# Middle rows of a Fourier transform as two stationary tiles of high and low parts, in a fused FFT and feed-forward kernel

## The chip, the cores and the metric

The kernel runs on one core of one Trainium2 chip. The metric is the device time in microseconds of one execution; three runs of the kernel before stand below. One execution was recorded by the hardware profiler. The five engines are TensorE (PE, its weight loads PEld), VectorE (DVE), ScalarE (ACT), GpSimd (POOL) and SyncE (SP, which issues transfers).

## The reference

```python
X = np.fft.fft(x, axis=1); X = np.fft.fft(X, axis=2)   # x: 8 batches x 3072 x 256, fp32
y = X.real.astype(np.float32).reshape(8 * 3072, 256)
h = y @ w_in                                           # 256 -> 2048
g = np.maximum(h, 0.0) + alpha * np.minimum(h, 0.0)    # alpha: one number per hidden unit
out = (g @ w_out).astype(np.float32)                   # 2048 -> 256
```

## The kernel before

The transform over 3072 positions is reduced by sums and differences of mirrored rows ("folds") to small products of folded rows with cosine and sine tables. The transform over the 256 features is not computed by itself: it is multiplied into the first weight matrix. The folded results go to a tile `X`, as a high and a low part of each number.

**The feed-forward steps.** Columns of the result are worked on in blocks of 386, 384 or 512; a batch from 1 to 6 has three blocks of 512, batch 7 four of 386. A step is one block with one of 16 slices of the hidden layer. `ffn1` makes six products into two PSUM banks (lines L804 to L806), VectorE and ScalarE apply the activation (L822, L830, L834, L777), `split_parts` makes a high part `hi` on ScalarE (L783) and a low part `lo` on GpSimd (L785), and `ffn2` adds twelve products to four accumulators (L902). `ffn1` runs three steps ahead of `ffn2`. At the end of a block `evacuate` copies two accumulators by ScalarE (L931) and two by VectorE (L929); the next block's first products overwrite them. All products of this pair are in `float32r`, of high by high, high by low and low by high parts.

**The transforms beside them.** While the steps of batch b run, the transforms of batch b + 1 are prepared and run. `r` counts the steps of a batch, 0 to 47 where it has three blocks. GpSimd and VectorE do the folds at r = 4 to 36. The four even units (`see`, `cee`, `ceo`, `seo`) follow at r = 38, 40, 41, 42, the rows of the odd units are turned (`turn_rows`: six ScalarE copies `part` at L515, two GpSimd sums, `aco` or `aso` at L517 and `odds` at L518) at r = 44 and 46, and the two odd units, of two transforms each, run at r = 0 and 3 of the next batch. So a batch has eight transforms, four in even and four in odd units.

**One transform (`dft`).** A transform has 384 folded rows in three tiles of 128 and writes two column halves, even and odd, of 193 (or 192) columns side by side in one PSUM bank. Tile 0 feeds the even half only, tile 2 the odd half only. The middle tile feeds both: its lower 64 rows the even half, its upper 64 the odd half, and the table of the middle has zeros elsewhere. Tiles 0 and 2 are multiplied in fp32, which the profile shows as two passes per product (L603). The middle of batches 2 to 7 is multiplied in `float32r` (L600): three products of both halves together, 386 or 384 columns wide, by the pairs (high rows, high table), (high rows, low table), (low rows, high table). Some transforms add a product of four rows kept apart, `zres` by `res` (L599, 194 columns).

**Where the parts come from.** `parts` makes a `float32r` copy on ScalarE (L576, tile `mh`) and subtracts it from the fp32 numbers on GpSimd (L577, tile `ml`). `mids` calls it for the rows of an even unit pair at r = 37 and of the odd units at r = 44 (`co`) and 46 (`so`), behind `turn_rows`, on two groups of 128 rows by 128 columns each. `parts_table` does the same for the six tables once, at six steps of batch 1 (`TABLE_STEPS`).

**Order.** The schedule is written by hand: every engine works its own queue in the order in which the program issues. In a step the order is `ffn1` of three steps ahead, `ffn2`, the ScalarE copies of `evacuate` if a block ends, the activation (`pair`), the VectorE copies of `evacuate`; then the steps' transform work, as `turn_rows` and `mids`. The four banks of the pool `pq` rotate between `ffn1` and the transforms.

Of the kernel before, what the change touches and what calls it, by code (L numbers as in the profile page):

```python
# [10 lines left out]
F32 = mybir.dt.float32  # L11
# [76 lines left out]
def _tables():  # L88
    p = PI.reshape(3, P)
    j, i2 = np.arange(193)[None, :], np.arange(192)[None, :]  # L90

    def four(full):
# [9 lines left out]
    seo = four(s)  # L102
# [9 lines left out]
        ee=np.concatenate([cee, see], 1), eo=np.concatenate([ceo, seo], 1),  # L112
        er=np.concatenate([rca, rsb], 1), feat=feat, ident=ident,
    )
    return {k: np.ascontiguousarray(v, dtype=np.float32) for k, v in out.items()}


# [29 lines left out]
def fft2_prelu_ffn(ctx: ExitStack, tc: tile.TileContext, t, outputs):  # L147
    nc = tc.nc
# [34 lines left out]
    ee = tabs.tile([P, 8, 193], F32, name="ee")  # L183
    eo = tabs.tile([P, 8, 192], F32, name="eo")
    er = tabs.tile([P, 8, 193], F32, name="er")


    wih, wil = wts.tile([P, KF, 2, P], F32R, name="wih"), wts.tile([P, KF, 2, P], F32R, name="wil")
# [375 lines left out]
        )  # L564


    TABS = dict(cee=(ee, 0), see=(ee, 4), ceo=(eo, 0), seo=(eo, 4), ca=(er, 0), sb=(er, 4))
    middle = {}

    def parts(key, n, rows, places):  # L570

        tag = key if key in TABS else key[0]
        two = middle[key] = [late.tile([P, n], F32R, tag=f"m{tag}{h}", name="m" + h) for h in "hl"]
        for i, v in enumerate(rows):
            hi, lo = (places(m, i) for m in two)
            S.activation(out=hi, in_=v, func=ACTF.Copy)  # L576
            G.tensor_tensor(out=lo, in0=v, in1=hi.bitcast(F32), op=ALU.subtract)  # L577

    def parts_table(kind):
        tab, at = TABS[kind]  # L580
        v = tab[:, at + 2:at + 4].rearrange("p k n -> p (k n)")
        parts(kind, v.shape[-1], [_pairs(v)], lambda m, _: _halves(m))

    def dft(kind, v, zr, m, mid=None, bank=None):

        ps = (bank or other_bank())[0:m]
        tab, at = TABS[kind]
        n = tab.shape[-1]
        even, odd = [(v[:, 0], tab[:, at])], [(v[:, 2], tab[:, at + 1])]
        if mid is None:  # L590
            even.append((v[:, 1], tab[:, at + 2]))
            if zr is not None:
                even.append((zr.bitcast(F32), res[:, 0:n].bitcast(F32)))
            odd.append((v[:, 1], tab[:, at + 3]))
        else:
            (fh, fl), (th, tl) = mid, middle[kind]
            for i, (lhsT, rhs) in enumerate(((fh, th), (fh, tl), (fl, th))):
                if i == 2 and zr is not None:
                    nc.tensor.matmul(out=ps[:, 0:n + 1], lhsT=zr, rhs=res, start=False, stop=False)  # L599
                nc.tensor.matmul(out=_pairs(ps[:, 0:2 * n]), lhsT=lhsT, rhs=_halves(rhs), start=(i == 0), stop=False)  # L600
        for o, terms in ((0, even), (n, odd)):
            for i, (lhsT, rhs) in enumerate(terms):
                nc.tensor.matmul(  # L603
                    out=ps[:, o:o + n], lhsT=lhsT, rhs=rhs, start=(mid is None and i == 0),
                    stop=(i == len(terms) - 1 and (o > 0 or mid is None)),
                )
        return ps, n, m

    def dft_early(kind, v, zr):

        ps = other_bank()
        tab, at = TABS[kind]
        n = tab.shape[-1]
# [3 lines left out]
        terms += [(n, v[:, 1], tab[:, at + 3]), (n, v[:, 2], tab[:, at + 1])]  # L617
        for i, (o, lhsT, rhs) in enumerate(terms):
            if i in (1, len(terms) - 1):
                yield ps, n, P  # L620
            nc.tensor.matmul(
                out=ps[:, o:o + n], lhsT=lhsT, rhs=rhs, start=(i in (0, len(terms) - 2)), stop=(i in (len(terms) - 3, len(terms) - 1)),
            )

    def odd_sums(ps, n, m):
        os = foldp.tile([P, 193], F32, tag="os", name="os", bufs=2)[0:m, 0:n]
        S.activation(out=os, in_=ps[:, n:2 * n], func=ACTF.Copy)  # L627
        return ps, os, n, m

    def butterfly(ps, n, m):  # L630
# [9 lines left out]

    def mids(b, nm):

        low, high = rows_of(b, nm)
        rows = [low[:, 1] if nm[1] == "e" else turned[nm][:, 1], high[:, 1]]
        parts(nm, 2 * P, rows, lambda m, i: m[:, i * P:(i + 1) * P])

    def mid_of(nm, i):
        return [m[:, i * P:(i + 1) * P] for m in middle[nm]] if nm in middle else None

    def unit_odd(b, nm):  # L650

# [439 lines left out]
    for b in range(NB):  # L1091
# [3 lines left out]
        for r in range(len(mine) * KF):  # L1095
# [118 lines left out]
```

## Time and profile before

| | us |
|---|---|
| median of three runs | 1643.32 (1641.93 to 1643.6) |
| the profiled execution, own time | 1642.61 |
| its span, first to last instruction | 1640.8 |
| TensorE busy | 1626.6 (99%) |
| VectorE, GpSimd, ScalarE busy | 1455.2 (89%), 1292.4 (79%), 1131.3 (69%) |

The granted TensorE clock is 0.999 of full speed over the span. A matmul's record is longer than the time for which it holds the stream: records of successive matmuls overlap, so it is the distance between their starts that counts. In a row of the timeline several instructions of one group are merged; "x4" is their count, and the time is from the first start to the last end. Engine names with PEld are weight loads.

### The profile page before, as it was taken

What the parts mean: (1) busy time and instruction counts of PE and PEld (TensorE: products, weight loads), DVE (VectorE), ACT (ScalarE), POOL (GpSimd) and SP (SyncE); (2) the same over time, 40 slices, a digit from 0 to 9 for tenths busy, and PEclk for the clock granted to TensorE, in tenths of its full rate; (3) what the DMA queues carried; (4) which work ended last, traced back from release to release, by engine and by line L of the source; (5) the groups of instructions that cost most, each with busy time, mean ns of one, the idle gap of its engine ahead of it and who ended that gap; (6) DMA issues with size and microseconds to landing.
All of it is one profiled execution on the core that took longest, in us unless ns stands there. A gap on an engine that the chain in (4) does not pass through costs nothing.

```text
span 1640.8 us, 25922 instructions
## 1 busy us (share of the span) xinstructions
PE 1626.6 (99%) x8132; PEld 1455.1 (89%) x8132; DVE 1455.2 (89%) x2483; ACT 1131.3 (69%) x2094; POOL 1292.4 (79%) x1306
## 2 busy tenths in 40 slices
PE   8999999999999999999999999999999999999998
PEld 6779999888888888888888888888888888899998
DVE  7979988999899998999889998899988999889997
ACT  6876677667676667766676666766667666677775
POOL 4688987888788888888877888788878888776665
PEclk9999999999999999999999999999999999999999
DMA  6410210011000120010100101001100010000000
GB/s 238 135 53 6 63 65 20 20 59 52 20 33 28 45 71 1 33 52 33 59 27 7 63 22 59 26 8 71 52 20 26 20 46 32 1 31 25 25 20 21
DMA packets 25531, 69.28 MB, mean 42 GB/s; under 512 B 5722, under 2 KB 8114, under 8 KB 25394
## 3 DMA queue, kind: packets, MB, share of 16 engines
q1 hardware_dynamic: 25090, 67.45, 11.6%
q8 instruction: 65, 1.06, 0.3%
q14 instruction: 72, 0.59, 0.1%
q10 hardware_dynamic: 304, 0.17, 0.0%
HBM read 42.34 MB, written 25.26 MB: 41 GB/s over the span
## 4 chain that ended last, share of the span: by engine, by line
PE 93%; DVE 2%; POOL 1%; ACT 1%; issue 1%; DVEq 0%; POOLq 0%; ACTq 0%
PE acc L902 57%; PE pq L804 10%; PE pq L806 10%; PE pq L805 10%; PE ps L603 3%; PE acc L876 2%; PE ps L600 1%; PE ps L376 1%; DVE d L830 1%; POOL lo L785 1%; DVE pf L822 0%; DVE d L777 0%; ACT pq L834 0%; ACT part L515 0%; ACT hi L783 0%
## 5 line engine op out<-in xcount | busy, mean ns | idle before, releaser
L785 POOL TENSOR_TENSOR lo<-d,hi 128x512 fp32r<-128x512 f32 (+2 forms) x804 | 971.5, 1225 | 284.2 <-ACT hi L783 255.3
L783 ACT ACTIVATE hi<-d 128x512 fp32r<-128x512 f32 (+2 forms) x804 | 483.0, 601 | 356.2 <-DVE d L777 307.5
L777 DVE SCALAR_TENSOR_TENSOR d<-d,sg,pq 128x512 f32<-128x512 f32 (+2 forms) x804 | 565.6, 703 | 11.6 <-ACT pq L834 11.6
L834 ACT ACTIVATE pq<-d,sga 128x512 f32<-128x512 f32 (+2 forms) x832 | 541.4, 653 | 45.2 <-DVE d L830 44.3
L830 DVE TENSOR_TENSOR d<-pf,pq 128x512 f32<-128x512 f32 (+2 forms) x832 | 530.7, 641 | 8.5 <-POOL lo L785 0.4
L902 PE MATMUL acc<-hi,h 128*128 128x512 f32 (+2 forms) x1604 | 455.3, 365 | 1.1 <-ACT o L931 1.0
L822 DVE SCALAR_TENSOR_TENSOR pf<-xbc,w,pq 128x512 f32<-128x512 f32 (+2 forms) x416 | 299.0, 719 | 108.7 <-PE pq L806 100.9
L902 PE MATMUL acc<-lo,h 128*128 128x512 f32 (+2 forms) x1604 | 391.9, 364 | 0.0
L902 PE MATMUL acc<-hi,l 128*128 128x512 f32 (+2 forms) x1604 | 391.9, 364 | 0.0
L902 PEld LDWEIGHTS acc<-hi,h 128*128 128x128 f32 x1604 | 297.3, 189 | 34.7 <-ACT o L931 3.6
L902 PEld LDWEIGHTS acc<-lo,h 128*128 128x128 f32 x1604 | 294.6, 189 | 30.9
L902 PEld LDWEIGHTS acc<-hi,l 128*128 128x128 f32 x1604 | 294.6, 189 | 30.8
L804 PE MATMUL pq<-X,wih 128*128 128x512 f32 (+2 forms) x832 | 314.2, 378 | 3.3 <-DVE d L777 3.2
L806 PE MATMUL pq<-X,wil 128*128 128x512 f32 (+2 forms) x832 | 302.1, 363 | 1.5 <-DVE wil L392 1.5
L805 PE MATMUL pq<-X,wih 128*128 128x512 f32 (+2 forms) x832 | 301.9, 363 | 0.1
L804 PEld LDWEIGHTS pq<-X,wih 128*128 128x128 f32 x832 | 157.0, 189 | 26.2 <-PE pq L806 3.1
L806 PEld LDWEIGHTS pq<-X,wil 128*128 128x128 f32 x832 | 157.1, 189 | 17.6 <-DVE wil L392 2.0
L805 PEld LDWEIGHTS pq<-X,wih 128*128 128x128 f32 x832 | 157.2, 189 | 16.1 <-DVE X L701 0.3
L423 POOL TENSOR_TENSOR raw<-raw 128x512 f32<-128x512 f32 (+1 forms) x112 | 97.7, 873 | 0.0
L638 DVE TENSOR_TENSOR y<-ps,os 128x193 f32<-128x193 f32 (+3 forms) x68 | 21.1, 352 | 31.2 <-ACT os L627 31.2
L344 POOL TENSOR_TENSOR w<-we,wm 128x512 int32<-128x512 int32 (+1 forms) x18 | 21.2, 1180 | 33.6 <-DVE wm L334 17.3
L931 ACT ACTIVATE o<-acc 128x512 f32<-128x512 f32 (+2 forms) x50 | 25.5, 561 | 21.7 <-PE acc L902 21.7
(172 smaller groups left out, 916.6 us busy)
## 6 DMA issues: line engine op xcount, KB each, us to landing
raw<-in_xh SPq DMA_DIRECT2D x42, 512.0 KB
out<-o SPq DMA_DIRECT2D x36, 512.0 KB
raw<-in_w SPq DMA_DIRECT2D x16, 512.0 KB
xbc<-xcd SPq DMA_DIRECT2D x18, 256.0 KB
out<-o SPq DMA_DIRECT2D x8, 386.0 KB
before<-in_xh SPq DMA_DIRECT2D x6, 512.0 KB
out<-o SPq DMA_DIRECT2D x6, 384.0 KB
er<-in_er SPq DMA_DIRECT2D x1, 772.0 KB
```

The costliest lines, as they stand in the source:

```text
L423: yield size, lambda o=o, i0=i0, i1=i1, op=op: e.tensor_tensor(out=o, in0=i0, in1=i1, op=op)
L603: nc.tensor.matmul(out=ps[:, o:o + n], lhsT=lhsT, rhs=rhs, start=(mid is None and i == 0), stop=(i == len(terms) - 1 and (o > 0 or mid is ...
L777: V.scalar_tensor_tensor(out=g, in0=d, scalar=sg[:, f:f + 1], in1=ad, op0=ALU.mult, op1=ALU.max)
L783: S.activation(out=hi, in_=d, func=ACTF.Copy)
L785: G.tensor_tensor(out=lo, in0=d, in1=hi.bitcast(F32), op=ALU.subtract)
L804: nc.tensor.matmul(out=out, lhsT=wih[:, f, q], rhs=xh, start=True, stop=False)
L805: nc.tensor.matmul(out=out, lhsT=wih[:, f, q], rhs=xl, start=False, stop=False)
L806: nc.tensor.matmul(out=out, lhsT=wil[:, f, q], rhs=xh, start=False, stop=True)
L822: V.scalar_tensor_tensor(out=_pairs(pf), in0=_halves(xbc[g]), scalar=w128[:, f:f + 1], in1=_pairs(ps[0]), op0=ALU.mult, op1=ALU.add,)
L830: V.tensor_tensor(out=d, in0=pf, in1=ps[1], op=ALU.add if i else ALU.subtract)
L834: S.activation(out=ad, in_=d, func=ACTF.Copy, scale=sga[:, f:f + 1])
L902: nc.tensor.matmul(out=out, lhsT=wt[:, o * P:(o + 1) * P], rhs=rhs, start=(f == 0 and n[o] == 0), stop=(f == KF - 1 and n[o] == 2),)
```

## The change

For batches 2 to 7 the middle tile is no longer one tile of high and one of low parts of all 128 rows. It becomes two stationary tiles, `me` and `mo`. `me` holds the high parts of the lower 64 rows in partitions 0 to 63 and their low parts in partitions 64 to 127; `mo` holds the high parts of the upper 64 rows in partitions 64 to 127 and their low parts in 0 to 63. Each table half becomes two tiles of 194 (192) columns: the high part of its 64 rows in both partition halves, and the low part in both. A column half is then two products, with the high and with the low table, and a transform has four products of half the columns in place of three of all. All four pairs of parts are in them. The odd half starts at column 194 of the bank (192 where n is 192), and the tables `ee` and `er` are padded with a column of zeros.

The copies and subtractions change with it: each works on 64 partitions, the subtraction reads one partition half and writes the other, an odd unit's middle takes four of each instead of two, an even one's two of each on 256 columns, and a table two of each per column half, at twelve steps of batch 1.

```diff
-    def parts_table(kind):
-        tab, at = TABS[kind]
-        v = tab[:, at + 2:at + 4].rearrange("p k n -> p (k n)")
-        parts(kind, v.shape[-1], [_pairs(v)], lambda m, _: _halves(m))
+    LOWER, UPPER = slice(0, 64), slice(64, 128)
+
+    def parts_table(kind, o):
+
+        tab, at, n = TABS[kind]
+        own, other = ((LOWER, UPPER), (UPPER, LOWER))[o]
+        m = [late.tile([P, n + n % 2], F32R, tag=f"m{kind}{o}{h}", name="m" + h) for h in "hl"]
+        middle.setdefault(kind, []).append(m)
+        v = _pairs(tab[own, at + 2 + o])
+        for rows in (own, other):
+            S.activation(out=_halves(m[0][rows]), in_=v, func=ACTF.Copy)
+        for rows in (own, other):
+            G.tensor_tensor(out=_halves(m[1][rows]), in0=v, in1=_halves(m[0][own]).bitcast(F32), op=ALU.subtract)
...
-            (fh, fl), (th, tl) = mid, middle[kind]
-            for i, (lhsT, rhs) in enumerate(((fh, th), (fh, tl), (fl, th))):
-                if i == 2 and zr is not None:
-                    nc.tensor.matmul(out=ps[:, 0:n + 1], lhsT=zr, rhs=res, start=False, stop=False)
-                nc.tensor.matmul(out=_pairs(ps[:, 0:2 * n]), lhsT=lhsT, rhs=_halves(rhs), start=(i == 0), stop=False)
...
+        w = n + n % 2
+        for o in range(2):
+            out, wide = ps[:, w * o:w * o + n], ps[:, w * o:w * o + w]
...
+                terms += [(_pairs(wide), mid[o], _halves(m)) for m in middle[kind][o]]
+                if o == 0 and zr is not None:
+                    terms.append((ps[:, 0:n + 1], zr, res))
+                terms.append((out, v[:, 2 * o], tab[:, at + o]))
+            for i, (at_, lhsT, rhs) in enumerate(terms):
+                nc.tensor.matmul(out=at_, lhsT=lhsT, rhs=rhs, start=(i == 0), stop=(i == len(terms) - 1))
...
     def mids(b, nm):
 
-        low, high = rows_of(b, nm)
-        rows = [low[:, 1] if nm[1] == "e" else turned[nm][:, 1], high[:, 1]]
-        parts(nm, 2 * P, rows, lambda m, i: m[:, i * P:(i + 1) * P])
+        two = [late.tile([P, 2, P], F32R, tag=f"m{nm[0]}{o}", name="m" + o) for o in "eo"]
+        middle[nm] = [m[:, ::-1] if nm == "se" else m for m in two]
+        if nm[1] == "e":
+            at = 4 if nm == "ce" else 5
+            groups = [(slice(0, 2), even[:, at:at + 3:2])]
+        else:
+            groups = [(0, turned[nm][:, 1]), (1, rows_of(b, nm)[1][:, 1])]
+        for k, v in groups:
+            for m, own, other in ((two[0], LOWER, UPPER), (two[1], UPPER, LOWER)):
+                S.activation(out=m[own, k], in_=v[own], func=ACTF.Copy)
+                G.tensor_tensor(out=m[other, k], in0=v[own], in1=m[own, k].bitcast(F32), op=ALU.subtract)
...
-    TABLE_STEPS = (7, 11, 18, 22, 26, 30)
+    TABLE_STEPS = (5, 7, 9, 11, 13, 18, 20, 22, 24, 26, 28, 30)
...
-                parts_table(list(TABS)[TABLE_STEPS.index(r)])
+                parts_table(list(TABS)[TABLE_STEPS.index(r) // 2], TABLE_STEPS.index(r) % 2)
```

## Rows read from the trace of the kernel before

**Rows 1.** The page: busy time by engine, and the chain that ended last.

```profile
PE 1626.6 (99%) x8132; PEld 1455.1 (89%) x8132; DVE 1455.2 (89%) x2483; ACT 1131.3 (69%) x2094; POOL 1292.4 (79%) x1306
...
PE 93%; DVE 2%; POOL 1%; ACT 1%; issue 1%; DVEq 0%; POOLq 0%; ACTq 0%
```

**Rows 2.** The chain of waits in order of time: start us, us, what, count.

```profile
461.16 2.59 PE acc L902 x12
...
465.05 2.85 PE acc L902 x12
...
1250.15 2.82 PE acc L902 x12
```

**Rows 3.** Timeline of TensorE: start us, us, engine, line, out<-in, [idle before].

```profile
1445.87 0.92 PE L902 MATMUL acc<-hi,h 128*128 128x386 f32 x2 [0.72 <-ACT o L931]
```

**Rows 4.** All instructions of line L600: count, ns min/median/max, first and last start, forms.

```profile
L600 PE MATMUL ps<-mh x48: 326/327/462, 423.9 to 1460.9; 128*128 128x386 f32 x36, 128*128 128x384 f32 x12
...
L600 PE MATMUL ps<-ml,mh x48: 326/327/327, 424.1 to 1461.2; 128*128 128x386 f32 x36, 128*128 128x384 f32 x12
```

**Rows 5.** Timeline of TensorE, the products of one transform.

```profile
432.86 0.33 PE L600 MATMUL ps<-mh 128*128 128x386 f32 x1
433.03 0.33 PE L600 MATMUL ps<-ml,mh 128*128 128x386 f32 x1
433.19 0.25 PE L599 MATMUL ps<-res,zres 128*128 128x194 f32 x1
433.28 0.35 PE L600 MATMUL ps<-mh,ml 128*128 128x386 f32 x1
433.46 0.82 PE L603 MATMUL ps<-ee,even 128*128 128x193 f32 x4
```

**Rows 6.** Timeline of TensorE's weight loads, the same transform.

```profile
433.19 0.19 PEld L600 LDWEIGHTS ps<-mh,ml 128*128 128x128 f32 x1
433.30 0.68 PEld L603 LDWEIGHTS ps<-ee,even 128*128 128x128 f32 x4
```

**Rows 7.** Timeline of TensorE behind the `co` pair of batch 2.

```profile
470.57 0.38 PE L806 MATMUL pq<-X,wil 128*128 128x512 f32 x1
470.79 0.44 PE L804 MATMUL pq<-X,wih 128*128 128x512 f32 x1
```

**Rows 8.** Timeline of GpSimd, r = 44 to 46 of batch 1's block.

```profile
455.88 0.46 POOL L577 TENSOR_TENSOR ml<-aco,mh 128x128 fp32r<-128x128 f32 x1
456.35 0.46 POOL L577 TENSOR_TENSOR ml<-odds,mh 128x128 fp32r<-128x128 f32 x1
456.87 5.02 POOL L785 TENSOR_TENSOR lo<-d,hi 128x512 fp32r<-128x512 f32 x4
461.90 1.02 POOL L517 TENSOR_TENSOR aso<-odds,part 128x384 f32<-128x384 f32 x1
```

**Rows 9.** Timeline of ScalarE at the boundary of batches 1 and 2.

```profile
463.92 0.31 ACT L576 ACTIVATE mh<-odds 128x128 fp32r<-128x128 f32 x1 [0.66 <-POOL odds L518]
464.14 1.07 ACT L931 ACTIVATE o<-acc 128x512 f32<-128x512 f32 x2
```

**Rows 10.** Timeline of TensorE at the same boundary.

```profile
464.88 0.86 PE L902 MATMUL acc<-hi,h 128*128 128x512 f32 x2
```

**Rows 11.** Timeline of GpSimd at r = 37 of batch 1.

```profile
422.83 1.72 POOL L577 TENSOR_TENSOR ml<-even,mh 128x128 fp32r<-128x128 f32 x4
```

**Rows 12.** Timeline of GpSimd at the start.

```profile
1.34 0.88 POOL L257 MEMSET ee<- 64x386 f32 x2
...
2.17 0.41 POOL L278 MEMSET zres<- 128x384 f32 x1
```

**Rows 13.** GpSimd's groups by line and form: count, busy us, mean ns, idle before.

```profile
L423 POOL TENSOR_TENSOR raw<-raw 128x256 f32<-128x256 f32 x84 | 61.7, 735 | 0.0
```

**Rows 14.** Stretches: us, then busy us (count) of PE, PEld, DVE, ACT, POOL; clock, DMA.

```profile
296.28:331.25 34.97, 34.97 (x164) 30.62 (x163) 32.61 (x51) 24.21 (x39) 31.64 (x29) 1.00 0.05 16
346.79:397.29 50.50, 50.50 (x236) 44.22 (x235) 47.03 (x73) 35.44 (x57) 45.62 (x42) 1.00 0.08 27
```

More of the change, by code (lines that the diff above doesn't have):

```diff
@@ L114, in _tables @@
     )
+    for k in ("ee", "er"):
+        out[k] = np.concatenate([out[k], np.zeros((P, 8, 1))], 2)
     return {k: np.ascontiguousarray(v, dtype=np.float32) for k, v in out.items()}
@@ L181, in fft2_prelu_ffn @@
     dummy = work.tile([P, 512], F32R, tag="hi0", name="dummy", bufs=3)
-    ee = tabs.tile([P, 8, 193], F32, name="ee")
+    ee = tabs.tile([P, 8, 194], F32, name="ee")
     eo = tabs.tile([P, 8, 192], F32, name="eo")
-    er = tabs.tile([P, 8, 193], F32, name="er")
+    er = tabs.tile([P, 8, 194], F32, name="er")
     wih, wil = wts.tile([P, KF, 2, P], F32R, name="wih"), wts.tile([P, KF, 2, P], F32R, name="wil")
@@ L564, in load_rows_384 @@
         )
-    TABS = dict(cee=(ee, 0), see=(ee, 4), ceo=(eo, 0), seo=(eo, 4), ca=(er, 0), sb=(er, 4))
+    TABS = dict(
+        cee=(ee, 0, 193), see=(ee, 4, 193), ceo=(eo, 0, 192), seo=(eo, 4, 192), ca=(er, 0, 193), sb=(er, 4, 193),
+    )
     middle = {}
[L570 to L577, printed above, removed]
@@ L584, in dft @@
     def dft(kind, v, zr, m, mid=None, bank=None):
         ps = (bank or other_bank())[0:m]
[L587 to L595, printed above, removed]
-            (fh, fl), (th, tl) = mid, middle[kind]
-            for i, (lhsT, rhs) in enumerate(((fh, th), (fh, tl), (fl, th))):
-                if i == 2 and zr is not None:
-                    nc.tensor.matmul(out=ps[:, 0:n + 1], lhsT=zr, rhs=res, start=False, stop=False)
-                nc.tensor.matmul(out=_pairs(ps[:, 0:2 * n]), lhsT=lhsT, rhs=_halves(rhs), start=(i == 0), stop=False)
@@ L601, in dft @@
[L601 to L606, printed above, removed]
+        tab, at, n = TABS[kind]
+        tab = tab[:, :, 0:n]
+        w = n + n % 2
+        for o in range(2):
+            out, wide = ps[:, w * o:w * o + n], ps[:, w * o:w * o + w]
+            terms = []
+            if mid is None:
+                terms += [(out, v[:, 2 * o], tab[:, at + o]), (out, v[:, 1], tab[:, at + 2 + o])]
+                if o == 0 and zr is not None:
+                    terms.append((out, zr.bitcast(F32), res[:, 0:n].bitcast(F32)))
+            else:
+                terms += [(_pairs(wide), mid[o], _halves(m)) for m in middle[kind][o]]
+                if o == 0 and zr is not None:
+                    terms.append((ps[:, 0:n + 1], zr, res))
+                terms.append((out, v[:, 2 * o], tab[:, at + o]))
+            for i, (at_, lhsT, rhs) in enumerate(terms):
+                nc.tensor.matmul(out=at_, lhsT=lhsT, rhs=rhs, start=(i == 0), stop=(i == len(terms) - 1))
@@ L611, in dft_early @@
         ps = other_bank()
-        tab, at = TABS[kind]
-        n = tab.shape[-1]
+        tab, at, n = TABS[kind]
+        tab = tab[:, :, 0:n]
         terms = [(0, v[:, 0], tab[:, at]), (0, v[:, 1], tab[:, at + 2])]
@@ L616, in dft_early @@
             terms.append((0, zr.bitcast(F32), res[:, 0:n].bitcast(F32)))
-        terms += [(n, v[:, 1], tab[:, at + 3]), (n, v[:, 2], tab[:, at + 1])]
+        w = n + n % 2
+        terms += [(w, v[:, 1], tab[:, at + 3]), (w, v[:, 2], tab[:, at + 1])]
         for i, (o, lhsT, rhs) in enumerate(terms):
@@ L626, in odd_sums @@
         os = foldp.tile([P, 193], F32, tag="os", name="os", bufs=2)[0:m, 0:n]
-        S.activation(out=os, in_=ps[:, n:2 * n], func=ACTF.Copy)
+        S.activation(out=os, in_=ps[:, n + n % 2:2 * n + n % 2], func=ACTF.Copy)
         return ps, os, n, m
@@ L641, in mids @@
     def mids(b, nm):
-        low, high = rows_of(b, nm)
-        rows = [low[:, 1] if nm[1] == "e" else turned[nm][:, 1], high[:, 1]]
-        parts(nm, 2 * P, rows, lambda m, i: m[:, i * P:(i + 1) * P])
+        two = [late.tile([P, 2, P], F32R, tag=f"m{nm[0]}{o}", name="m" + o) for o in "eo"]
[3 more added lines that the diff above has]
+            groups = [(slice(0, 2), even[:, at:at + 3:2])]
+        else:
+            groups = [(0, turned[nm][:, 1]), (1, rows_of(b, nm)[1][:, 1])]
[3 more added lines that the diff above has]
+                G.tensor_tensor(out=m[other, k], in0=v[own], in1=m[own, k].bitcast(F32), op=ALU.subtract)
     def mid_of(nm, i):
-        return [m[:, i * P:(i + 1) * P] for m in middle[nm]] if nm in middle else None
+        return [m[:, i] for m in middle[nm]] if nm in middle else None
     def unit_odd(b, nm):
```

## The prediction, made before the changed kernel was run

> **What bounds the kernel now.** I read the page first: its busy times and its chain of waits [rows 1]. TensorE is busy for 99% of the span and 93% of the chain is its own work, so a change pays only by what it takes from TensorE's stream, and costs only where TensorE is made to wait. Next, the chain in order of time [rows 2]: the twelve second-layer products of a 512-column step take 2.59 us, 0.216 us each, step after step. At 465.05 they take 2.85. Five such rows stand in the trace, one at each of the first five batch boundaries (465, 661, 857, 1053 and 1250 us), each about 0.25 us too long. The sixth boundary idles longer, for 0.72 us in its row and behind one name: L931, ScalarE's copy of the finished accumulator [rows 3]. Between the boundaries TensorE is full. So two things are to be priced: the transforms' products, and what the new splits do to the copy at the boundary.
>
> **The products.** There are 48 transforms with a middle (six batches by eight), three `float32r` products each, 36 transforms at 386 columns and 12 at 384 [rows 4]. In the stream [rows 5] such products start 0.165 us apart (432.86, 433.03, 433.19), so three cost 0.49 us. The change puts four products of 194 (or 192) columns in their place. The trace holds one product of that width, L599 with 194 columns: from its start to the start of the second product behind it are 0.27 us, of which the 386-column one takes 0.165, so L599 holds the stream for 0.11 us, not half of 0.165. The load row tells why [rows 6]: the load that begins with L599 is followed 0.11 us later by the next load. Every product brings a load of 128 columns, also where the same stationary tile is used twice running (L600 has 48 loads for `ps<-mh` and 48 for `ps<-ml,mh` [rows 4]). A product shorter than 0.11 us costs 0.11.
>
> The Trainium skill says it too (TensorE: Matmul & The Clock Gate, section "LDWEIGHTS (loading the stationary operand)"): a load takes its column count over 1.2, 107 ns for 128 columns, however few rows are in use; the load rows agree. The same page's section "Back-to-back issue gap" gives columns over 2.4 plus 2.5 ns for the product alone, an estimated 83 ns at 194 columns; the stream here goes by the load.
>
> Four products are then 0.44 us against 0.49, and 0.05 us goes per transform, 2.4 us over 48. The fp32 products (two a transform) and L599 keep their number and width. Not all 2.4 us stay. Behind the `co` pair (r = 0 of a batch) TensorE already waits for a bank: the L804 row at 470.79 is 0.44 us long where its neighbours have 0.38 [rows 7]. That bank comes free by the chain that starts at the boundary, so there the 0.1 us a batch, 0.6 in all, only lengthens a wait. Kept: even units 24 x 0.05 = 1.2, `so` pairs 12 x 0.05 = 0.6, together 1.8 us.
>
> **The splits at the boundary.** Each middle of an odd unit is now written by four ScalarE copies and four GpSimd subtractions on 64 rows instead of two and two on 128. GpSimd's run [rows 8]: the subtractions `ml` at 455.88 and 456.35 (r = 44), then four `lo` in one unbroken run of 5.02 us from 456.87, then `aso` at 461.90, 0.01 us after it, and `odds` behind it. ScalarE [rows 9] copies `mh<-odds` at 463.92, after 0.66 us of waiting for that `odds`, and the accumulator copies follow in the same queue at 464.14, 1.07 us for both. TensorE's second product of the new block waits for the second one: its pair takes 0.86 us from 464.88, where two unhindered ones would end within 0.216 + 0.38 = 0.60 [rows 7, 10]. The whole chain thus runs through GpSimd, and nothing in it has slack: what is added on GpSimd at r = 44 arrives at TensorE at r = 48.
>
> Added there, by rows: a subtraction of 128 elements issued back to back costs 0.42 us (four `ml` in 1.72 us at 422.83 [rows 11], one alone is 0.46 long [rows 8]: 1.26 / 3). I take that for 64 partitions too, because a memset of 386 elements on 64 partitions takes as long as one of 384 on 128: two in 0.88 us against 0.41 for one [rows 12]. Four from 455.88 let `lo` start at 455.88 + 4 x 0.42 = 457.56, not 456.87: 0.69 us late. `aso` and `odds` inherit it. Then ScalarE has two copies instead of one behind `odds`; the second costs the 0.22 us between 463.92 and 464.14 [rows 9]. The accumulator copy comes 0.69 + 0.22 = 0.91 us later, and TensorE, which had no slack to it, waits 0.91 us more. The chain starts behind steps that TensorE itself paces, so an earlier TensorE shifts it all alike. Six boundaries (b = 1 to 6): 5.5 us. Behind them the queues and TensorE are late by the same amount, so nothing is won back.
>
> Bounds of this term. Below: half tiles could run beside each other on GpSimd, so that two cost what one does; then only ScalarE's copies count, once at r = 44 before `lo` and once before the accumulator copy, 0.22 + 0.22 = 0.44 a boundary, 2.6 us. Above: the result lies in the other 64 partitions, which no row shows; at the nearest dearer row, 0.735 us for 256 elements [rows 13], two extra and two dearer subtractions make `lo` late by 4 x 0.735 - 0.99 = 1.95 and the boundary by 2.2, 13 us over six. I take 0.91, the value by the rows of the same operation and size.
>
> **The other edits.** At r = 37 the even middles become 256-element instructions on 64 rows: four subtractions at up to 0.735 us for four in 1.72, 1.2 us more on GpSimd. No accumulator copy follows them for ten steps, and the products of `see` need the second half only behind two products and two fp32 ones; I cost it at nothing, up to 0.1 us a batch (0.6 us) if it is late. The tables (b = 1, twelve steps instead of six): twice the copies and subtractions at about half the columns, some 0.6 us each (between 0.46 for 128 elements and 0.735 for 256), 24 of them for six of some 1.1 (0.735 x 386 / 256), 8 us more on GpSimd, off the boundaries. GpSimd is idle for 3.3 us in the stretch of its first five steps and 4.9 in that of the other seven [rows 14], against some 3.9 and 4.2 to be added, so a backlog stays under two steps: nothing, or 1 us if that cover is gone. Padding the tables to 194 columns adds 0.5% to two loads, nothing.
>
> **Sum.** 5.5 - 1.8 = +3.7 us. On the profiled execution's own 1642.61 us that is 1646.3; its span is 1640.8 and 1.8 us lie around it, untouched. The median of the runs shown, 1643.32, is 0.7 above that execution, so for the median I say 1647.0.
>
> **Rivals.**
> - *GpSimd overlaps the halves.* The splits alternate between the lower and the upper 64 rows. If GpSimd works on both at once, two halves cost one whole, the boundary loses 0.44 us, and the sum is 2.6 - 1.8 = +0.8 us, 1644.1. Against it: the two half memsets, on opposite halves, took 0.88 us together [rows 12]; they read nothing, so it stays open. Chance 0.17. For it stands a rule of the Trainium skill (GPSIMD Engine Reference, section "2.1 Instruction dispatch"): each of the engine's cores serves 16 partitions and starts the next instruction as soon as its own share is done.
> - *The load does not limit.* Two products running on one stationary tile, or other loads, might pass at 0.083 us (half of 0.165), the stream's own pace. A transform then saves 0.49 - 0.33 = 0.16, the kept 36 save 5.8, and the sum is 5.5 - 5.8 = -0.3 us, 1643.0: not slower. It decides if TensorE's starts inside a pair lie under 0.09 us apart. Against it [rows 6]. Chance 0.10.
> - *The boundary hides it.* If GpSimd's queue has slack between 455.9 and 461.9 that the rows do not show, all 2.4 us land: 1640.9. The unbroken run speaks against it. Chance 0.06.
> - *The narrow product streams slower.* L599 reads its columns in a row, the new products read pairs 97 apart, and fp32 at 193 columns takes two passes of 0.165 [rows 5]. At 0.165 a product a transform loses 0.17, 8 us in all, plus the boundary: +13.5, 1657. So would the dear subtraction above. Chance of either 0.10.
> - Forecast: 0.57.
>
> **How the numbers follow.** What a measurement of this kernel can tell from no change is 0.2%, 3.3 us. The forecast's +3.7 sits just past it; within its own spread of some 1.5 us, it is slower by that two times in three. Slower: 0.57 x 0.65 + 0.10 = 0.47, and 0.49 with the tables' share. Faster by 3.3: the hidden boundary alone gives -2.4 and both favourable prices together 2.6 - 5.8 = -3.2, so only a part of each: 0.05. Same: 0.46. The range reaches from just under the load rival, 1642.6, to 1651.0, part of the way to the dear subtraction.
>
> **What would show it.** Loads of a pair 0.11 us apart, four products and two fp32 passes in sequence; the first `lo` behind the `co` splits 0.7 us later than before, counted from `aco`; the boundary's twelve products at about 3.7 us instead of 2.85, with L931 named; the L804 behind `co` longer by 0.1. It is wrong if the boundary rows stay at 2.85, or if loads come closer than 0.11.

## The result, and the profile after

| | before | after |
|---|---|---|
| median, six runs each | 1643.05 (1641.93 to 1643.62) | 1653.36 (1652.88 to 1653.53) |
| span of the profiled execution | 1640.8 | 1651.1 |

The ratio is 1.0063, with an interval of 1.005 to 1.0076: slower by 10.3 us, where +3.7 was forecast. The direction held and the size did not. The time lies 2.4 us above the upper end of the range.

First the chain of the kernel after by engine, from its page:

```profile
PE 85%; DVE 2%; POOL 2%; issue 1%; ACT 1%; DVEq 0%; POOLq 0%; ACTq 0%
```

TensorE was 93% of the span before [rows 1], and is 85% now. Most of that drop is no loss: followed back from the end, the chain of the kernel after reaches to 155 us, that of the kernel before to 23, and what it doesn't reach counts for no engine. From 158 us on, where both stand, TensorE is 97.5% of the chain before and 94.0% after; GpSimd rises from 7 us to 30, VectorE from 17 to 32. What TensorE waited for, summed by releaser (us in total, times, longest), in the kernel after and then in the kernel before:

```profile
PE pq L813 <- DVE d L786: 6.6, 15, 0.9
PE acc L911 <- ACT o L940: 5.5, 7, 1.3
```

```profile
PE pq L804 <- DVE d L777: 3.2, 7, 0.9
...
PE acc L902 <- ACT o L931: 1.0, 2, 0.7
```

L813 is L804 of before, and L940 is L931. Of the eight new bank waits six lie at the boundaries, one in batch 1 (401 us) and one 7 us behind the last `co` pair; the five new waits for the accumulator's copy lie at the first five boundaries, where it was too short to be listed before. Waits of under 0.15 us are not in these sums. The chain in order of time shows a boundary from within (start us, us, what; in the same stretch of before, every piece was TensorE's [rows 2]):

```profile
457.28 0.23 POOL me L654
...
463.16 1.01 POOL aso L519
464.17 0.98 POOL odds L520
...
465.50 0.31 ACT mo L653
...
465.83 0.61 ACT o L940
```

From the half subtractions on, the chain is GpSimd's, with its four `lo`, `aso` and `odds`, then ScalarE's half copy and the accumulator copy. The way was forecast; its length was not. GpSimd there, from the timeline (start us, us, engine, line, operation, form, count); the rows answer to [rows 8]:

```profile
454.90 1.01 POOL L520 TENSOR_TENSOR odds<-odds,part 128x384 f32<-128x384 f32 x1
455.99 0.45 POOL L654 TENSOR_TENSOR me<-aco,me 64x128 fp32r<-64x128 f32 x1
456.52 0.46 POOL L654 TENSOR_TENSOR mo<-aco,mo 64x128 fp32r<-64x128 f32 x1
...
458.12 5.01 POOL L794 TENSOR_TENSOR lo<-d,hi 128x512 fp32r<-128x512 f32 x4
463.16 1.01 POOL L519 TENSOR_TENSOR aso<-odds,part 128x384 f32<-128x384 f32 x1
```

Each of the four half subtractions (two of them are shown) is as long as a whole one was (0.45 to 0.46), but they start 0.53 apart, with 0.08 of nothing between one's end and the next one's start. The `lo` run starts at 458.12, where it was 456.87 [rows 8]: 1.25 us late, and `aso` inherits it (463.16 for 461.90). ScalarE at the boundary, answering to [rows 9]:

```profile
465.17 0.31 ACT L653 ACTIVATE me<-odds 64x128 fp32r<-64x128 f32 x1 [0.33 <-POOL odds L520]
465.50 0.31 ACT L653 ACTIVATE mo<-odds 64x128 fp32r<-64x128 f32 x1
465.83 1.09 ACT L940 ACTIVATE o<-acc 128x512 f32<-128x512 f32 x2
```

From the first copy behind `odds` to the accumulator's copy are 0.66 us, where they were 0.22 [rows 9]: two steps of 0.33, again with a gap (0.02) in each. The accumulator copy thus starts 1.69 us late (464.14 to 465.83), 1.25 by GpSimd and 0.44 by ScalarE. TensorE, answering to [rows 7, 10]:

```profile
460.13 0.38 PE L815 MATMUL pq<-X,wil 128*128 128x512 f32 x1
460.93 0.45 PE L813 MATMUL pq<-X,wih 128*128 128x512 f32 x1 [0.42 <-DVE d L786]
461.22 0.38 PE L814 MATMUL pq<-X,wih 128*128 128x512 f32 x1
...
465.32 0.38 PE L815 MATMUL pq<-X,wil 128*128 128x512 f32 x1
466.49 0.97 PE L911 MATMUL acc<-hi,h 128*128 128x512 f32 x2 [0.78 <-ACT o L940]
467.29 1.03 PE L911 MATMUL acc<-hi,l 128*128 128x512 f32 x4
...
472.22 0.38 PE L815 MATMUL pq<-X,wil 128*128 128x512 f32 x1
472.68 0.45 PE L813 MATMUL pq<-X,wih 128*128 128x512 f32 x1
```

Starts of such products are 0.22 apart unhindered. Here L815 to L813 at 460.93 takes 0.80, and L813 to L814 0.29: 0.65 us lost. L815 to L911 at 466.49 takes 1.17, and the pair behind it 0.80 for 0.43: 1.32 lost. That is 1.97 a boundary for 0.26 before, +1.71. The first part came at a place that the prediction did not name: VectorE's L839 waits 0.84 us for a late `lo` and hands the delay on through L786 to a bank. The two together are the 1.7 us by which the copy is late, so the first part is taken to be a share of that delay and not a cost of its own. Behind the `co` pair, L815 to L813 at 472.68 takes 0.46 and the next step about 0.29: 0.32 lost, for some 0.06 before [rows 7]. Five boundaries are alike; at the sixth TensorE idles 0.95 us for a bank, for nothing before, and 1.25 us for L940, for 0.72 [rows 3].

The products: first, from the chain of the kernel before, the time of one transform's fp32 passes; then the rows of the kernel after, answering to [rows 5], and their weight loads, answering to [rows 6]:

```profile
468.50 0.65 PE ps L603 x4
```

```profile
469.98 0.38 PE L606 MATMUL ps<-mh,mo 128*128 128x194 f32 x1
470.20 0.28 PE L606 MATMUL ps<-ml,mo 128*128 128x194 f32 x1
470.31 0.52 PE L606 MATMUL ps<-er,aco 128*128 128x193 f32 x2
...
471.08 0.38 PE L606 MATMUL ps<-mh,mo 128*128 128x194 f32 x1
```

```profile
424.08 0.19 PEld L606 LDWEIGHTS ps<-ml,me 128*128 128x128 f32 x1
424.19 0.30 PEld L606 LDWEIGHTS ps<-ee,even 128*128 128x128 f32 x2
```

From `mo` to `mo`, four narrow products and four fp32 passes take 1.10 us; before, the `float32r` products took 0.49 [rows 5] and the four passes 0.65, together 1.14. A transform saves about 0.05, as forecast. The loads begin 0.11 apart.

A count over all of TensorE's products checks the split. Each is given the time for which it holds the stream (0.11 us for a narrow one, 0.216 for 512 columns, 0.165 for 386, in proportion for others, and twice for the two passes of fp32); the rest, up to the next start, is waiting. Holding sums to 1611.3 us before and 1608.9 after, -2.4. Waiting sums to 23.1 and 35.9, +12.8: 2.1 for each of the six boundaries with the steps around it (12.6), 0.8 in batch 1, and -0.7 in the start-up. Within 0.1 they add up to the +10.3 between the spans. The start-up is taken for chance and not for a part of the change: in the traces of the runs below it ends between 0.8 us earlier and 1.5 us later than in the kernel before.

### The profile page after: what moved, and what is told of

It is laid out like the page before. It is cut to its first block, busy times and chain, and to the rows that moved or that the text cites. A ratio compares the mean times of both kernels' runs of the same rounds, so it can differ in the third digit from the quotient of the medians.

```text
span 1651.1 us, 26120 instructions
## 1 busy us (share of the span) xinstructions
PE 1627.0 (99%) x8180; PEld 1450.7 (88%) x8180; DVE 1459.5 (88%) x2483; ACT 1152.0 (70%) x2136; POOL 1320.2 (80%) x1348
## 4 chain that ended last, share of the span: by engine, by line
PE 85%; DVE 2%; POOL 2%; issue 1%; ACT 1%; DVEq 0%; POOLq 0%; ACTq 0%
PE acc L911 54%; PE pq L813 9%; PE pq L815 9%; PE pq L814 9%; PE ps L606 4%; POOL lo L794 1%; DVE d L839 1%; DVE d L786 1%; DVE pf L831 0%; POOL aso L519 0%; POOL odds L520 0%; ACT o L940 0%; PE acc L896 0%; ACT mo L653 0%; POOL mo L654 0%
## 5 line engine op out<-in xcount | busy, mean ns | idle before, releaser
L786 DVE SCALAR_TENSOR_TENSOR d<-d,sg,pq 128x512 f32<-128x512 f32 (+2 forms) x804 | 566.0, 704 | 19.5 <-ACT pq L843 19.5
L839 DVE TENSOR_TENSOR d<-pf,pq 128x512 f32<-128x512 f32 (+2 forms) x832 | 531.2, 642 | 14.4 <-POOL lo L794 6.8
L911 PE MATMUL acc<-hi,h 128*128 128x512 f32 (+2 forms) x1604 | 455.8, 365 | 5.5 <-ACT o L940 5.5
L911 PE MATMUL acc<-hi,l 128*128 128x512 f32 (+2 forms) x1604 | 392.0, 364 | 0.0
L911 PE MATMUL acc<-lo,h 128*128 128x512 f32 (+2 forms) x1604 | 392.0, 364 | 0.0
L911 PEld LDWEIGHTS acc<-hi,h 128*128 128x128 f32 x1604 | 297.3, 189 | 40.7 <-ACT o L940 10.1
L813 PE MATMUL pq<-X,wih 128*128 128x512 f32 (+2 forms) x832 | 314.9, 379 | 7.2 <-DVE d L786 6.6
L911 PEld LDWEIGHTS acc<-lo,h 128*128 128x128 f32 x1604 | 294.6, 189 | 30.9
L911 PEld LDWEIGHTS acc<-hi,l 128*128 128x128 f32 x1604 | 294.5, 189 | 30.9
L815 PE MATMUL pq<-X,wil 128*128 128x512 f32 (+2 forms) x832 | 302.0, 363 | 1.5 <-DVE wil L394 1.5
L814 PE MATMUL pq<-X,wih 128*128 128x512 f32 (+2 forms) x832 | 301.9, 363 | 0.0
L813 PEld LDWEIGHTS pq<-X,wih 128*128 128x128 f32 x832 | 157.1, 189 | 34.6 <-PE pq L815 11.2
L815 PEld LDWEIGHTS pq<-X,wil 128*128 128x128 f32 x832 | 157.1, 189 | 17.6 <-DVE wil L394 2.1
L814 PEld LDWEIGHTS pq<-X,wih 128*128 128x128 f32 x832 | 157.3, 189 | 15.8 <-DVE X L710 0.3
L425 DVE TENSOR_TENSOR raw<-raw 128x256 f32<-128x256 f32 (+1 forms) x56 | 41.1, 734 | 0.0
```

What stands on the lines that cost most here:

```text
L425: yield size, lambda o=o, i0=i0, i1=i1, op=op: e.tensor_tensor(out=o, in0=i0, in1=i1, op=op)
L786: V.scalar_tensor_tensor(out=g, in0=d, scalar=sg[:, f:f + 1], in1=ad, op0=ALU.mult, op1=ALU.max)
L813: nc.tensor.matmul(out=out, lhsT=wih[:, f, q], rhs=xh, start=True, stop=False)
L814: nc.tensor.matmul(out=out, lhsT=wih[:, f, q], rhs=xl, start=False, stop=False)
L815: nc.tensor.matmul(out=out, lhsT=wil[:, f, q], rhs=xh, start=False, stop=True)
L839: V.tensor_tensor(out=d, in0=pf, in1=ps[1], op=ALU.add if i else ALU.subtract)
```

## The experiments

**The question.** The half instructions cost more than their length. One theory is the *count*: there are twice as many instructions, and only that matters. The other is the *place*: an instruction that works at other partitions than the one ahead of it in its queue does not overlap with that one. Rivals to both: the subtraction is dear because it *crosses*, reading one half and writing the other; and the *products* cost part of the 10 us.

### The count at either place: dup_low, dup_up

The kernel before, with a second copy and a second subtraction of 64 rows to the same tiles, for the odd units alone, on the lower (dup_low) or the upper rows (dup_up, `slice(64, 128)`).

```diff
-            S.activation(out=hi, in_=v, func=ACTF.Copy)
-            G.tensor_tensor(out=lo, in0=v, in1=hi.bitcast(F32), op=ALU.subtract)
+            again = [slice(0, P)] + [slice(0, 64)] * (key in ("co", "so"))
+            for p in again:
+                S.activation(out=hi[p], in_=v[p], func=ACTF.Copy)
+            for p in again:
+                G.tensor_tensor(out=lo[p], in0=v[p], in1=hi[p].bitcast(F32), op=ALU.subtract)
```

> The kernel before, with the copy and the subtraction of each odd unit's middle issued a second time on the lower 64 rows (start partition 0): four and four as in the change, same products as before. Theory A (an instruction of ScalarE or GpSimd overlaps its predecessor only if it starts at the same partition; a change of start costs about 0.11 us on either): no start changes here, so the second copies cost 0.22 us and the second subtractions 0.42, the boundary is 0.9 us later and the time 1643.05 + 5.5 = 1648.5. Theory B (half-width instructions are dear by themselves): subtractions 0.53 apart, about 1653. Theory C (count alone, the forecast's price): 1648.5 as well.

> As the run before it, but the second copies and subtractions are on the upper 64 rows (start partition 64), and nothing crosses from one half to the other. Theory A: start changes at every one of them, copies 0.33 apart and subtractions 0.53, with an idle gap of about 25 ns on ScalarE and 60 to 80 ns on GpSimd ahead of each; boundary about 1.6 to 1.7 us later, 1643.05 + 10 to 11.5 = 1653 to 1654.5. Theory B: the same as the run on the lower rows. Theory C (count alone): 1648.5. Theory D (crossing from one half to the other is dear): 1648.5.

Measured: dup_low 1650.54 (ratio 1.0046 [1.0034, 1.0059]), dup_up 1653.71 (1.0067 [1.0054, 1.0079]). dup_up alone, without a single changed product, is as slow as the whole change. dup_low came out 2 us dearer than expected, and its timeline shows why it is not a clean test: its second instructions write where their own engine has just written, and wait for that (a gap of 0.03 us on ScalarE, 0.08 on GpSimd). Those of dup_up wait in the same way, so it isn't one either. So dup2, below, gives them tiles of their own.

### The same halves in another order: order

The kernel after, with the two halves swapped in every second group, so that some neighbours in a queue have the same place.

```diff
+        both = ((two[0], LOWER, UPPER), (two[1], UPPER, LOWER))
...
-            for m, own, other in ((two[0], LOWER, UPPER), (two[1], UPPER, LOWER)):
+            for m, own, other in both[::-1] if k == 1 or nm == "ce" else both:
```

> The changed kernel with the second group's two tiles in the other order (me, mo, mo, me instead of me, mo, me, mo), so that one change of start partition less lies on each engine in each odd unit. Theory A: the second of two neighbours with the same start follows with no gap, 0.42 on GpSimd and 0.22 on ScalarE; the chain to the accumulator copy is about 0.1 us shorter on GpSimd and 0.1 on ScalarE, 6 x 0.2 = 1.3 us: 1652.1. Theories B, C, D: no change, 1653.4.

Measured: 1650.73 (1.0047 [1.0035, 1.006]), 2.6 us below the change, where 1.3 was expected: besides 0.23 us of the chain at each boundary (below), the wait behind `co` shrank, from 0.32 us to 0.21 at the first five. GpSimd in it, then ScalarE, then TensorE behind the `co` pair:

```profile
456.50 0.46 POOL L655 TENSOR_TENSOR mo<-aco,mo 64x128 fp32r<-64x128 f32 x1
456.92 0.47 POOL L655 TENSOR_TENSOR mo<-odds,mo 64x128 fp32r<-64x128 f32 x1
457.46 0.46 POOL L655 TENSOR_TENSOR me<-odds,me 64x128 fp32r<-64x128 f32 x1
```

```profile
465.04 0.31 ACT L654 ACTIVATE mo<-odds 64x128 fp32r<-64x128 f32 x1 [0.33 <-POOL odds L520]
465.37 0.31 ACT L654 ACTIVATE me<-odds 64x128 fp32r<-64x128 f32 x1
465.58 1.05 ACT L941 ACTIVATE o<-acc 128x512 f32<-128x512 f32 x2
```

```profile
471.91 0.38 PE L816 MATMUL pq<-X,wil 128*128 128x512 f32 x1
472.26 0.45 PE L814 MATMUL pq<-X,wih 128*128 128x512 f32 x1
```

The two `mo` that now follow one another start 0.42 apart and overlap; `me`, at another place, follows 0.54 behind. On ScalarE the copy of the lower rows, which begin where whole tiles begin, is followed by L941 after 0.21; the step from upper to lower takes 0.33. One kernel, the same operation and size, two prices, by the place of the neighbour. Behind `co`, L816 to L814 takes 0.35 where the kernel after has 0.46; the wait is not back to the 0.06 of the kernel before.

### The products alone: prod

The kernel after, with `mids` making whole-row parts as the kernel before does.

```diff
...
-        for k, v in groups:
-            for m, own, other in ((two[0], LOWER, UPPER), (two[1], UPPER, LOWER)):
-                S.activation(out=m[own, k], in_=v[own], func=ACTF.Copy)
-                G.tensor_tensor(out=m[other, k], in0=v[own], in1=m[own, k].bitcast(F32), op=ALU.subtract)
+        low, high = rows_of(b, nm)
+        for k, v in enumerate((low[:, 1] if nm[1] == "e" else turned[nm][:, 1], high[:, 1])):
+            S.activation(out=two[0][:, k], in_=v, func=ACTF.Copy)
+            G.tensor_tensor(out=two[1][:, k], in0=v, in1=two[0][:, k].bitcast(F32), op=ALU.subtract)
```

> The changed kernel with its four products and its tables, but the rows' tiles made by one copy and one subtraction of all 128 rows per group as before (so the tiles hold high parts alone and low parts alone, and the output is not the reference's). If the splits at the boundary are the whole loss: stalls at the boundary back to 0.26 us, the products' 2.4 us won less what the wait behind the co pair takes back, and the tables' 0.8 us of stalls left: 1643.05 - 1.8 + 0.8 = 1642. If part of the loss is in the products themselves: above 1644.

Measured: 1641.77 (0.9995 [0.9986, 1.0004]), as expected; the interval holds no change. The boundary is nearly back to what it was:

```profile
464.49 0.38 PE L810 MATMUL pq<-X,wil 128*128 128x512 f32 x1
464.71 0.83 PE L906 MATMUL acc<-hi,h 128*128 128x512 f32 x2
465.38 1.03 PE L906 MATMUL acc<-hi,l 128*128 128x512 f32 x4
```

L906 starts 0.22 behind L810, as if nothing were awaited; its pair takes 0.67 for 0.43. So the products cost nothing of the 10 us, and the row splits carry the loss.

### Count and place with spare tiles: dup2_low, dup2_up

The kernel before again, the second copy and subtraction of 64 rows going to spare tiles. The cut shows dup2_low; dup2_up has `slice(64, 128)`.

```diff
+        if key in ("co", "so"):
+            x = [late.tile([P, P], F32R, tag=f"x{n_}", name=f"x{n_}") for n_ in range(3)]
+            spare = [(x[0], x[1]), (x[2], x[0])]
...
-            S.activation(out=hi, in_=v, func=ACTF.Copy)
-            G.tensor_tensor(out=lo, in0=v, in1=hi.bitcast(F32), op=ALU.subtract)
+            pairs = [(hi, lo, slice(0, P))]
+            if key in ("co", "so"):
+                pairs.append((*spare[i], slice(0, 64)))
+            for h, l, p in pairs:
+                S.activation(out=h[p], in_=v[p], func=ACTF.Copy)
+            for h, l, p in pairs:
+                G.tensor_tensor(out=l[p], in0=v[p], in1=h[p].bitcast(F32), op=ALU.subtract)
```

> The kernel before with the odd units' second copies and subtractions on the lower 64 rows again, now into spare tiles, so that no second one has to wait for the one that it would overwrite (in the first version it did, and a gap of 32 or 78 ns stood there whatever the start partition). Theory A (only a change of start partition forfeits the overlap): no gap, subtractions 0.42 and copies 0.22 apart, the boundary some 0.9 us later, 1643.0 + 5.5 = 1648.5. If half width costs by itself: 1651 or more.

> The same with the spare work on the upper 64 rows, nothing crossing. Theory A: gaps of about 25 ns on ScalarE and 60 to 80 ns on GpSimd at each change of start, copies 0.33 and subtractions 0.53 apart, boundary 1.5 to 1.6 us later than before, 1652.5 to 1653.5. If count alone matters, or crossing, or width: the same as on the lower rows.

Measured: dup2_low 1647.98 (1.0034 [1.0021, 1.0046]), dup2_up 1653.63 (1.0065 [1.0052, 1.0079]). GpSimd in dup2_low, and in dup2_up:

```profile
455.98 0.46 POOL L585 TENSOR_TENSOR ml<-aco,mh 128x128 fp32r<-128x128 f32 x1
456.40 0.47 POOL L585 TENSOR_TENSOR x<-aco,x 64x128 fp32r<-64x128 f32 x1
...
457.65 5.04 POOL L793 TENSOR_TENSOR lo<-d,hi 128x512 fp32r<-128x512 f32 x4
```

```profile
457.42 0.47 POOL L585 TENSOR_TENSOR ml<-aco,mh 128x128 fp32r<-128x128 f32 x1
457.96 0.46 POOL L585 TENSOR_TENSOR x<-aco,x 64x128 fp32r<-64x128 f32 x1
...
459.58 5.01 POOL L793 TENSOR_TENSOR lo<-d,hi 128x512 fp32r<-128x512 f32 x4
```

The same number of the same instructions on 64 rows: 0.42 apart where all begin at partition 0, 0.54 where they alternate between 0 and 64, and 5.65 us between the two times. Neither crosses. dup2_low is what the prediction priced: four at 0.42 and one more copy at 0.22. Its TensorE waits 0.9 us more at a boundary than the kernel before, which was the forecast, and its time is 5.1 us above that of the kernel before on its chip (about 1642.9), where 5.5 stood in the sum for six boundaries.

One difference besides the place remains between the two. In the trace of dup2_up every GpSimd instruction of these splits whose place changes also waits for a semaphore that GpSimd itself raises, and so does the `lo` behind them; in dup2_low half of the second subtractions wait for it, and no gap stands ahead of those. So on GpSimd this pair alone can't tell the place from such a wait. What tells them apart are steps that don't wait for it: in the kernel after and in `order` that is every subtraction of a split but the first, 0.53 to 0.54 apart where the place changes and 0.42 where it doesn't, and one more in nocross, below. On ScalarE the steps of dup2_up are 0.33 long as well, and most of them wait for no semaphore of ScalarE's own.

### Without crossing: nocross

The kernel after, the subtraction reading and writing the same rows.

```diff
-                G.tensor_tensor(out=m[other, k], in0=v[own], in1=m[own, k].bitcast(F32), op=ALU.subtract)
+            for m, hi, rows in ((two[0], two[1], UPPER), (two[1], two[0], LOWER)):
+                G.tensor_tensor(out=m[rows, k], in0=v[rows], in1=hi[rows, k].bitcast(F32), op=ALU.subtract)
```

> The changed kernel with each subtraction kept within its own 64 partitions (the low parts of the other 64 rows are written, so the output is not the reference's). Theory A: start partitions change as before, so the subtractions stay 0.53 apart and the time 1653. Theory D (crossing is what costs): 0.42 apart, and about 1650.

Measured, in two runs: 1651.99 (1.0054 [1.0035, 1.0072]). Its subtractions:

```profile
456.37 0.46 POOL L655 TENSOR_TENSOR me<-aco,mo 64x128 fp32r<-64x128 f32 x1
456.89 0.46 POOL L655 TENSOR_TENSOR mo<-aco,me 64x128 fp32r<-64x128 f32 x1
...
457.95 0.45 POOL L655 TENSOR_TENSOR mo<-odds,me 64x128 fp32r<-64x128 f32 x1
458.37 1.29 POOL L795 TENSOR_TENSOR lo<-d,hi 128x512 fp32r<-128x512 f32 x1
```

They are 0.52 to 0.53 apart without crossing too, so crossing is not the price. Nor is a wait: by the trace the `mo` at 456.89 waits for no semaphore, and 0.06 us lie ahead of it all the same. The last step is the exception that supports the theory: `mo` here reads and writes the lower rows, `lo` behind it begins at partition 0 as well, and they are 0.42 apart. With the shorter step ahead of that `mo` it makes the chain on GpSimd 0.13 us shorter, 0.8 in six boundaries, of the 1.4 us by which this kernel is below the changed one; the rest lies within what two runs can tell.

One table holds this together: from the start of `odds` to the first `lo` on GpSimd at r = 44, and from ScalarE's first copy behind the next `odds` to its accumulator copy, at the boundary of batches 1 and 2. The values are differences of starts, as shown above or in the same stretch of the trace:

| | GpSimd, us | ScalarE, us | median, us |
|---|---|---|---|
| before (two whole) | 1.96 | 0.22 | 1643.05 |
| dup2_low (four, all from partition 0) | 2.63 | 0.42 | 1647.98 |
| order (four, one neighbour pair alike) | 3.11 | 0.54 | 1650.73 |
| nocross (four, upper and lower in turn) | 3.09 | 0.65 | 1651.99 |
| dup2_up (four, 0 and 64 in turn) | 3.13 | 0.67 | 1653.63 |
| after (four, lower and upper in turn) | 3.22 | 0.66 | 1653.36 |

### The splits off the boundary: after_spread, before_spread

If the boundary's chain is the loss, moving the odd units' splits off it must give it back, in either kernel. `co` is turned at r = 43 and split at r = 45; `so` is turned at r = 47, behind the accumulator copies, and split at r = 1 of the next batch. The kernel before got the same edit.

```diff
+            if b > 1 and r == 1:
+                mids(b, "so")
...
-                for nm, at in zip(("se", "ce", "co", "so"), (52, 52, 60, 62) if b == 0 else (37, 37, 44, 46)):
+                for nm, at in zip(("se", "ce", "co", "so"), (52, 52, 60, 62) if b == 0 else (37, 37, 43, 47)):
...
-                        if b:
+                        elif b:
...
+                if b and r == 45:
+                    mids(b + 1, "co")
```

> The changed kernel with the odd units' work taken off the way to the accumulator copy: rows of co turned at r = 43 and split at 45, rows of so turned at r = 47 behind the accumulator copies, and split at r = 1 of the next batch. If the loss is the chain through GpSimd to that copy: the boundary's stall goes (0 to 0.1 us), the bank wait ahead of it too, all 2.4 us of the products land, and the tables' 0.8 us of stalls stay: 1639.5 to 1641.5, faster than before. If the dearer splits cost by their own time wherever they stand: still above 1648.

> The kernel before with the same moves of the odd units' work. The boundary's 0.26 us go: 1643.0 - 1.6 = 1641.4. The run beside it should then lie 1 to 2 us lower (products 2.4 us less, tables 0.8 us of stalls more). If the moves do more than free the boundary, the two differ otherwise.

Measured: after_spread 1639.98 (0.9983 [0.9974, 0.9992]), before_spread 1641.04 (0.9988 [0.9979, 0.9997]). TensorE at the boundary in after_spread:

```profile
465.66 0.38 PE L815 MATMUL pq<-X,wil 128*128 128x512 f32 x1
465.88 0.59 PE L911 MATMUL acc<-hi,h 128*128 128x512 f32 x2
```

L911 starts 0.22 behind L815 (1.17 in the kernel after), and its pair is 0.59 long, for 0.97. The same half splits, with the same gaps, cost nothing at the boundary: 13.4 us between two orders of one program. In the kernel before the same moves were worth 1.9. What the change itself is then worth, 1641.04 - 1639.98 = 1.1 us, is less than the two intervals can separate.

### A version that beats both: best, before_spread2

after_spread with the order of `order`, and the twelve table steps moved away from the two places of batch 1 where a bank had been late.

```diff
-    TABLE_STEPS = (5, 7, 9, 11, 13, 18, 20, 22, 24, 26, 28, 30)
+    TABLE_STEPS = (3, 4, 9, 12, 14, 17, 20, 25, 28, 33, 35, 36)
```

> The changed kernel with the odd units' work spread as in the run after_spread, the second group's tiles in the order mo, me, and the twelve table steps moved to steps of batch 1 in which GpSimd has idle time (3, 4, 9, 12, 14, 17, 20, 25, 28, 33, 35, 36). If batch 1's stalls (0.8 us between 300 and 420 us) come from the tables' splits crowding GpSimd, they go: 1640.0 - 0.8 = 1639.2. If they come from something else that the tables do, they stay and the time is 1640.0.

> The kernel before with the moves alone, once more, beside the run above on one chip: 1641.0, some 1.8 us above it (products 2.4 us less, the wait behind co takes up to 0.6 back).

Measured: best 1639.40 (0.998 [0.9971, 0.9989]), before_spread2 1640.85 (0.9987 [0.9978, 0.9996]). Both beat the kernel before and the kernel after; that `best` beats `before_spread2` is not shown, as the intervals overlap. The 1639.2 that was forecast was met by luck. The waits at 315 and 401 us went, 0.8 us of TensorE's time, but a new one came at r = 38, 0.7 us with the one behind it: the split of `see` ends too late for TensorE. That the table steps 35 and 36, ahead of it in GpSimd's queue, make it late is likely and not shown. So the moved tables gained some 0.1 us and not 0.8, and the rest of the 0.6 us between the medians of after_spread and `best` lies within their spread:

```profile
423.58 0.35 PE L606 MATMUL ps<-mh,me 128*128 128x194 f32 x1 [0.20 <-POOL me L655]
```

## Why the prediction missed, step by step

- **The products: right.** -2.4 us of holding, as forecast; 0.11 a product, set by the load. The Trainium skill (TensorE: Matmul & The Clock Gate, section "LDWEIGHTS (loading the stationary operand)") has 107 ns for 128 columns, however few rows are used, and the load rows agree. prod, without the row splits, came out 1.3 us lower in the median and 1.6 in the span, where 1.8 was forecast for the products. In its trace the tables' waits (0.8 us more) and the start-up (0.8 less) cancel, so 1.6 is what the products left there.
- **The splits at the boundary: the step that failed.** The chain was the right one, and it had no slack, as said. The terms were too small: 0.69 us on GpSimd measured 1.25, and 0.22 on ScalarE measured 0.44. The sentence at fault is "I take that for 64 partitions too": the 0.42 came from four neighbours that all begin at partition 0 [rows 11], and the 0.22 from a whole copy before a whole copy [rows 9]. Both prices hold for 64 rows, as dup2_low shows, and neither holds where the place changes from one instruction to the next. 0.91 a boundary became 1.71.
- **The row that told.** The half memsets [rows 12] were read as "as long as", and they are as long: each is 0.41. But two of them take 0.88 for 0.82, a gap of 0.06 that whole tiles do not show. The second of them is on the lower rows, and the `zres` behind it, from partition 0 too, starts 0.05 us before its end [rows 12]: the rule stood in the kernel before. The prediction named the other place as unknown and bounded it by 13 us, then drew the range only part of the way there; that bound would have held it.
- **The `co` wait:** priced at 0.1 a batch for the shorter products, measured 0.25 more (0.32 for 0.06). prod, with the products and without the row splits, has 0.09 more, the price that was given; the rest comes with the splits, which this term left out. `order`, with 0.23 less on the chain, has 0.14 more.
- **The tables: nothing, or 1 us.** Measured 0.8. A pair of table halves takes 1.44 us on GpSimd, 0.72 each and not 0.6: 0.68 for one, longer than was priced, and a gap of 0.08 between them:

```profile
313.76 1.44 POOL L585 TENSOR_TENSOR ml<-ee,mh 64x194 fp32r<-64x194 f32 x2
```

  TensorE then waits for banks behind it (the kernel after, at 401 us: L815 to L813 takes 0.53 for 0.22):

```profile
400.78 0.38 PE L815 MATMUL pq<-X,wil 128*128 128x512 f32 x1
401.31 0.48 PE L813 MATMUL pq<-X,wih 128*128 128x512 f32 x1 [0.15 <-DVE d L786]
```

- **r = 37:** next to nothing, as forecast: from the first product of `see` to the next first-layer product are 1.00 us in the kernel after and 0.97 in prod, whose splits at r = 37 are whole: 0.03 a batch, within the 0.1 that was allowed.
- **The rivals.** *GpSimd overlaps the halves* is refuted: lower and upper halves start 0.53 apart, further than two whole ones. The rule named beside it (the Trainium skill, GPSIMD Engine Reference, section "2.1 Instruction dispatch") is not borne out by any row here. *The load does not limit* is refuted by loads 0.11 apart. *The boundary hides it* is refuted by 1.71. *The narrow product streams slower* is refuted by prod. Its second half, the dear subtraction, is what came, at some three quarters of its price (1.71 of 2.2 a boundary).

## What to carry to other kernels

Price an instruction by its start to the next one's start, in the order in which it will stand in its queue: splitting a full-height instruction into lower and upper halves doubled the count and also took the overlap between neighbours. Before adding such work to a chain without slack, look for a place behind the point that the chain releases; moving it by one to three steps was worth 13.4 us here, while the change it served was worth about one. Where halves can't be avoided, issue those with the same rows next to each other.

## What the runs showed of the hardware

- Neighbours in one queue that begin at the same partition overlap: 0.42 us from start to start for GpSimd subtractions 0.46 long, 0.22 for ScalarE copies 0.31 long. Where the next one begins at the other half (0 to 64, or back), they don't, and a gap is added: 0.52 to 0.54 on GpSimd, 0.33 on ScalarE. Other places than 0 and 64 were not tried. A change in what is written suffices: in a table's pair, both subtractions read the same rows and write different ones, and 0.06 to 0.08 us lie between them; in six of the twelve pairs the second waits for no semaphore (0.06). Whether a change in what is read suffices as well is open: in the kernel after, `lo` stands 0.53 behind an `mo` that wrote from partition 0 but read from 64, but that `lo` also waits for GpSimd's own semaphore.
- 64 rows cost what 128 do: 0.46 us for a subtraction of 128 elements at either height; for a copy 0.31 at 128 rows and 0.29 to 0.31 at 64.
- An instruction that waits for its own engine's last write has about the same gap: 0.08 us on GpSimd and 0.03 on ScalarE in dup_low, where its place is that of its neighbour.
